# A gated linear-attention and GeGLU kernel rewritten: feature weights folded on chip, numerators issued between the feed-forward matmuls

## The chip, the cores and the metric

The kernel runs on one core of a Trainium2 chip. The metric is the device time of one execution in microseconds (us), as a median over several runs. The one kept profile of the kernel before is of its slow kind: its span of 387.4 us and granted clock of 0.965 are those of its runs near 389 us, while its fastest runs (383 us) had 0.973. Its stages may therefore be some 4 to 6 us too long in sum; in which of them was not measured. "TensorE" is the matrix engine (PE in the profile, PEld its weight loads), "VectorE" is DVE, "ScalarE" is ACT, "GpSimd" is POOL, and SP is the engine whose queue (SPq) issues most transfers. A fast run is one that is not over 1.5% above the fastest of the same kernel; only fast runs enter the ratios.

## The reference

Two branches share one input of 2048 tokens and 640 features, and a sigmoid gate per token mixes them. Branch A is linear attention with 32 heads of 20 features; its feature map is a pair of softmaxes of a small per-head product. Branch B is a feed-forward block with a hidden width of 1728.

```python
qkv = x @ wqkv                                   # q, k, v: 32 heads of 20
pq, pk = q @ w_phi[h], k @ w_phi[h]              # 20 x 20 per head
phi = concat(softmax(p), softmax(-p))            # for pq and pk
kv  = einsum("bhsf,bhsd->bhfd", phi_k, v)        # state: sums over all tokens
z   = phi_k.sum(tokens)
o   = (phi_q @ kv) / (phi_q @ z + 1e-6)          # numerator / denominator
a   = o @ wo
b   = (gelu_tanh(x @ w_gate) * (x @ w_up)) @ w_down
out = g * a + (1 - g) * b                        # g = sigmoid(x . gate_w)
```

The state `kv` needs all tokens, so no numerator can start before the last token's `phi_k`. Branch B depends on none of this.

## The kernel before

It works in three stages with a fence between them: A builds the state, B computes numerators and divides, C runs the feed-forward block and both output products. Heads stand in six groups (five of 6 heads, one of 2), so that a group's 120 features fit 128 rows.

For q, it projects to a feature-major tile, copies it out of PSUM, multiplies by a block-diagonal `w_phi`, and takes two exponentials (k is treated alike in stage A, with a token-major result):

```python
def emit_qT_group(self, b, g):                     # 5 matmuls of 512 columns, then a copy
    ...                                            # (cut)
    sc.compute("act", lambda e: e.activation(self.qTb[0:P, slot, g, :], self.ps[0:P, colQT:colQT + BT], AF.Copy), ...)

def emit_pq_group(self, b, g):
    sc.compute("pe", lambda e: e.matmul(self.ps[0:P, colPQ:colPQ + BT],
        self.BD6[0:P, g, 0:P], self.qTb[0:P, qslot, g, :], start=True, stop=True), ...)
    for s, scale in ((0, 1.0), (1, -1.0)):
        sc.compute("act", lambda e: e.activation(self.eq_ap(b, s, g, ...), self.ps[0:P, colPQ:colPQ + BT], AF.Exp, scale=scale), ...)
```

In stage B each of 16 tiles of 128 tokens gets 12 numerator matmuls, then 24 matmuls of 2 or 6 columns for the softmax denominators and for `phi_q @ z`, then a chain of VectorE operations:

```python
for s in (0, 1):
    for g in range(NG):                            # numerators
        matmul(ps[:, c0:c0 + nh * DA], eq(b, s, g)[tile], self.KVsb[0:P, s, g, 0:nh * DA])
for s in (0, 1):
    for g in range(NG):                            # two narrow products per group
        matmul(ps[:, d0:d0 + nh], eq(b, s, g)[tile], self.G6[0:P, 0:nh])
        matmul(ps[:, z0:z0 + nh], eq(b, s, g)[tile], self.KVz[0:P, s, g, 0:nh])
# emit_tile_dve: 8 small operations on [128, 32], 4 products into O1 and O2, GpSimd adds them into Otm
```

In stage C every chunk of 128 hidden features takes 10 matmuls of 512 columns, and GELU is spelled out:

```python
act(gb, ps_gate, AF.Copy);  act(sq, ps_gate, AF.Square, scale=SQC3);  act(up, ps_up, AF.Copy, scale=0.5)
dve(cube, sq * gb);  dve(u, cube + gb)
act(th, u, AF.Tanh, scale=CT)
dve(h1, (th + 1.0) * gb);  dve(hT, up * h1)
```

The output products of a token block stand between the chunks of the next block, so `hT` has two buffers. `Otm` is transposed on TensorE, five 128x128 transposes per token tile.

The softmax here doesn't subtract the row's maximum and nothing guards it: scores larger than these inputs give would overflow.

## Time and profile before

The median was 384.99 us over three runs (382.83 to 389.44).

First the profile page of the kernel before, its rows of busy tenths. Each digit is the busy share of one of 40 equal slices of the span (9.7 us each); PEclk is the clock granted to TensorE in tenths of full speed.

```profile
PE   2799999974788797669999999999999999999896
DVE  0109999967896969966886155383334751553600
ACT  4157767577164645028996477595555964785522
PEclk9999999999698989589999999999999999999999
```

Up to its last slices, the right half is a row of nines for TensorE at full clock. The left half is not, from the ninth slice on.

Then the stages of the kernel before, from the view of busy time by windows: window, its length, busy us of each engine (instructions), mean granted clock, DMA share, GB/s.

```profile
0.00:14.37 14.37, 4.62 (x26) 2.84 (x26) 1.61 (x6) 4.10 (x5) 5.93 (x28) 1.00 0.69 198
14.37:100.10 85.73, 74.68 (x594) 42.62 (x604) 63.70 (x129) 54.01 (x106) 6.28 (x7) 0.98 0.37 114
100.10:170.90 70.80, 56.90 (x698) 34.60 (x706) 58.94 (x217) 28.61 (x54) 21.95 (x16) 0.85 0.01 2
172.50:384.00 211.50, 208.47 (x1204) 102.86 (x1228) 105.04 (x224) 141.90 (x270) 0.00 (x0) 0.99 0.04 13
```

The columns after the length are PE, PEld, DVE, ACT, POOL. In the last window, the feed-forward stage, TensorE is busy for 208.5 of 211.5 us while ScalarE is busy for 142 and VectorE for 105. In the window of stage B above it, TensorE is busy for 56.9 of 70.8 us and VectorE for 58.9. Neither is full: in the view of waits TensorE stands still there for 4.8 us until VectorE's O products are done and for 6.4 us until ScalarE is (exponentials and q's copies), and VectorE for 6.4 us until TensorE is.

The chain of waits of the kernel before shows the spacing (start, length, what), here two consecutive groups of five gate and up matmuls:

```profile
194.96 1.08 PE psum_arena L892 x5
196.03 1.08 PE psum_arena L886 x5
```

Five matmuls of 512 columns take 1.08 us, 216 ns each. The Trainium skill, "TensorE: Matmul & The Clock Gate", § Back-to-back issue gap, gives N/2.4 + 2.5 ns for N columns, 215.8 ns, as the gap of single matmuls; the trace agrees. "Busy" in the group lines below is the union of overlapping matmuls, so a mean of 380 ns there is the length of one matmul through the pipeline and not its cost.

Last, groups of instructions of the kernel before (line, engine, operation, tiles, shapes, count | busy us, mean ns | idle before and its releasers):

```profile
L754 PE MATMUL psum_arena<-KVz,Eq 128*128 128x6 bf16 x160 | 10.8, 166 | 0.0
L798 DVE TENSOR_TENSOR O_56<-psum_arena,RH 128x480 bf16<-128x480 f32 x16 | 10.4, 651 | 0.0
L734 PE MATMUL psum_arena<-KVsb,Eq 128*128 128x126 bf16 x160 | 14.0, 229 | 4.8 <-DVE O_56 L798 3.3 <-DVE O_57 L803 1.5
L932 DVE SCALAR_TENSOR_TENSOR h1s<-ths,gbs 128x512 bf16<-128x512 bf16 x52 | 36.0, 692 | 82.4 <-ACT ths L931 81.2
L931 ACT ACTIVATE ths<-us 128x512 bf16<-128x512 bf16 x52 | 32.6, 629 | 0.0
```

The third line shows numerators waiting for the O products that empty their PSUM banks. The fourth shows VectorE idle for 82 us before its GELU step: the engines of the elementwise chain wait; TensorE is idle for only 3 of the 211.5 us.

### The profile page before, as it was taken

The page shows a single profiled execution, that of the slowest core. Times are in us where ns is not written, and L with a number is a line of the kernel's source. Part 1 is how long each engine was busy: PE and PEld are TensorE (multiplying, and loading weights), DVE is VectorE, ACT ScalarE, POOL GpSimd, SP SyncE. Part 2 cuts the span into 40 slices and gives each one's busy share as a digit, 9 for nine tenths or more (in the row PEclk, how much of TensorE's full clock was granted, in tenths as well). Part 3 has the DMA queues.
Part 4 walks back from the last instruction along what each step waited for, and adds up shares of the span by engine and source line. Part 5 has one row for each costly group of instructions (what it writes and reads, how often), then busy time and mean ns, then how long its engine had stood idle before and what let it go on. Part 6 is the DMA issues. An engine that isn't in the chain of part 4 may idle for free.

```text
span 387.4 us, 6518 instructions
## 1 busy us (share of the span) xinstructions
PE 344.7 (89%) x2519; PEld 182.9 (47%) x2562; DVE 229.3 (59%) x574; ACT 230.6 (60%) x437; POOL 34.5 (9%) x51
## 2 busy tenths in 40 slices
PE   2799999974788797669999999999999999999896
PEld 1246565542454555524444544445555445444453
DVE  0109999967896969966886155383334751553600
ACT  4157767577164645028996477595555964785522
POOL 6001210000022423420000000000000000000000
PEclk9999999999698989589999999999999999999999
DMA  8445981000000000000000000000000000000010
GB/s 253 95 97 164 339 311 45 2 0 2 0 3 2 2 1 3 2 0 2 0 0 3 17 19 17 19 0 18 18 17 2 17 3 17 19 17 19 0 36 34
DMA packets 15241, 15.60 MB, mean 40 GB/s; under 512 B 9882, under 2 KB 13146, under 8 KB 15210
## 3 DMA queue, kind: packets, MB, share of 16 engines
q1 hardware_dynamic: 13610, 7.73, 7.0%
q0 software_dynamic: 1600, 7.46, 5.7%
q8 instruction: 20, 0.33, 0.4%
q14 instruction: 11, 0.09, 0.1%
HBM read 10.59 MB, written 2.62 MB: 34 GB/s over the span
## 4 chain that ended last, share of the span: by engine, by line
PE 57%; DVE 11%; ACT 8%; issue 2%; POOLq 0%; ACTq 0%; DVEq 0%
PE psum_arena L961 15%; PE psum_arena L886 13%; PE psum_arena L892 12%; PE psum_arena L974 6%; PE psum_arena L654 5%; ACT Eq L688 4%; DVE O_56 L798 2%; DVE O_57 L803 2%; DVE h1s L932 2%; PE psum_arena L945 2%; ACT ths L931 1%; PE psum_arena L520 1%; ACT qTb L661 1%; DVE hT L934 1%; PE psum_arena L734 1%
## 5 line engine op out<-in xcount | busy, mean ns | idle before, releaser
L932 DVE SCALAR_TENSOR_TENSOR h1s<-ths,gbs 128x512 bf16<-128x512 bf16 (+1 forms) x56 | 38.7, 691 | 83.0 <-ACT ths L931 81.8
L886 PE MATMUL psum_arena<-xT,wg_sb 128*128 128x512 bf16 (+1 forms) x274 | 70.6, 387 | 4.1 <-ACT sqs L901 3.5
L892 PE MATMUL psum_arena<-xT,wu_sb 128*128 128x512 bf16 (+1 forms) x274 | 69.1, 382 | 0.2
L961 PE MATMUL psum_arena<-wd_sb,hT 128*128 128x512 bf16 (+3 forms) x439 | 64.9, 298 | 2.0 <-DVE hT L934 1.5
L961 PEld LDWEIGHTS psum_arena<-wd_sb,hT 128*128 128x128 bf16 x448 | 34.2, 98 | 32.2 <-issue 4.0
L899 ACT ACTIVATE gbs<-psum_arena 128x512 bf16<-128x512 f32 (+1 forms) x56 | 33.6, 601 | 19.8 <-POOL Otm L808 18.9
L886 PEld LDWEIGHTS psum_arena<-xT,wg_sb 128*128 128x128 bf16 (+1 forms) x280 | 26.8, 100 | 36.6 <-ACT sqs L901 3.8
L892 PEld LDWEIGHTS psum_arena<-xT,wu_sb 128*128 128x128 bf16 (+1 forms) x280 | 27.9, 100 | 33.8 <-issue 1.6
L948 ACT ACTIVATE goTs<-psum_arena 128x640 bf16<-128x640 bf16 x16 | 11.2, 703 | 53.1 <-PE psum_arena L945 53.1
L931 ACT ACTIVATE ths<-us 128x512 bf16<-128x512 bf16 (+1 forms) x56 | 35.1, 628 | 1.5 <-DVE us L918 1.5
L554 DVE TENSOR_REDUCE DkRk<-Ek 128x64 f32<-128x1280 bf16 x16 | 23.6, 1472 | 20.0 <-ACT Ek L547 20.0
L654 PE MATMUL psum_arena<-xT,wqkv_sb 128*128 128x512 bf16 x111 | 31.5, 431 | 4.0 <-ACT Eq L688 3.3
L904 ACT ACTIVATE ups<-psum_arena 128x512 bf16<-128x512 f32 (+1 forms) x56 | 33.7, 601 | 0.6 <-PE psum_arena L892 0.6
L901 ACT ACTIVATE sqs<-psum_arena 128x512 bf16<-128x512 f32 (+1 forms) x56 | 33.6, 601 | 0.0
L661 ACT ACTIVATE qTb<-psum_arena 128x512 bf16<-128x512 f32 x24 | 14.3, 597 | 32.4 <-PE psum_arena L654 29.7
L808 POOL TENSOR_TENSOR Otm<-O_56,O_57 128x640 bf16<-128x640 bf16 x16 | 22.3, 1395 | 86.7 <-DVE O_57 L803 86.7
L501 PE MATMUL psum_arena<-xT,wqkv_sb 128*128 128x512 bf16 x114 | 29.0, 402 | 0.7 <-DVE BD L465 0.4
L520 PE MATMUL psum_arena<-wqkv_sb,xT 128*128 128x512 bf16 (+1 forms) x157 | 26.3, 297 | 3.0 <-ACT gcol L543 2.9
L688 ACT ACTIVATE Eq<-psum_arena 128x512 bf16<-128x512 f32 x48 | 24.8, 606 | 2.1 <-PE psum_arena L681 2.1
L916 DVE TENSOR_TENSOR cubes<-sqs,gbs 128x512 bf16<-128x512 bf16 (+1 forms) x56 | 23.4, 417 | 3.5 <-ACT sqs L901 3.5
L562 DVE TENSOR_TENSOR Ek<-Ek,DkRk 128x640 bf16<-128x640 bf16 x32 | 25.0, 821 | 0.6
L918 DVE TENSOR_TENSOR us<-cubes,gbs 128x512 bf16<-128x512 bf16 (+1 forms) x56 | 23.8, 424 | 1.9
(77 smaller groups left out, 407.2 us busy)
## 6 DMA issues: line engine op xcount, KB each, us to landing
out_dram<-outsb SPq DMA_DIRECT2D x16, 160.0 KB, 1.8
wd_sb<-in_B_w_down_dram POOLq DMA_DIRECT2D x1, 2080.0 KB, 10.6
wqkv_sb<-in_A_wqkv_dram SPq DMA_DIRECT2D x1, 1600.0 KB, 8.6
wg_sb<-in_B_w_gate_dram POOLq DMA_DIRECT2D x1, 1200.0 KB, 7.6
wu_sb<-in_B_w_up_dram POOLq DMA_DIRECT2D x1, 1200.0 KB, 7.4
wg_sb<-in_B_w_gate_dram POOLq DMA_DIRECT2D x1, 960.0 KB, 7.2
wu_sb<-in_B_w_up_dram POOLq DMA_DIRECT2D x1, 960.0 KB, 5.6
wqkv_sb<-in_A_wqkv_dram SPq DMA_DIRECT2D x1, 800.0 KB
```

Source lines behind the costliest of these rows:

```text
L501: sc.compute("pe", lambda e, kt=kt, last=last, b=b, g=g, col=col: e.matmul(ps[0:P, col:col + BT], self.wqkv_sb[:, kt, D + self.w_col[g]:D ...
L520: sc.compute("pe", lambda e, kt=kt, c0=c0, n=n, last=last, tok0=tok0: e.matmul(ps[:, c0:c0 + n], self.xT[:, kt, tok0:tok0 + P], self.wqkv_ ...
L654: sc.compute("pe", lambda e, kt=kt, last=last, b=b, g=g: e.matmul(self.ps[0:P, colQT:colQT + BT], self.wqkv_sb[:, kt, self.w_col[g]:self.w ...
L688: sc.compute("act", lambda e, s=s, scale=scale, b=b, g=g, colPQ=colPQ: e.activation(self.eq_ap(b, s, g, 0, P, slice(0, BT)), self.ps[0:P, ...
L886: sc.compute("pe", lambda e, kt=kt, last=last, rows=rows, c=c, colg=colg, b=b: e.matmul(ps[0:rows, colg:colg + BT], self.wg_sb[:, kt, c * ...
L892: sc.compute("pe", lambda e, kt=kt, last=last, rows=rows, c=c, colu=colu, b=b: e.matmul(ps[0:rows, colu:colu + BT], self.wu_sb[:, kt, c * ...
L899: sc.compute("act", lambda e, rows=rows, colg=colg: e.activation(gb, ps[0:rows, colg:colg + BT], AF.Copy), reads=[("psb", bg)], writes=[(" ...
L901: sc.compute("act", lambda e, rows=rows, colg=colg: e.activation(sq, ps[0:rows, colg:colg + BT], AF.Square, scale=SQC3), reads=[("psb", bg ...
L904: sc.compute("act", lambda e, rows=rows, colu=colu: e.activation(up, ps[0:rows, colu:colu + BT], AF.Copy, scale=0.5), reads=[("psb", bu)], ...
L931: sc.compute("act", lambda e: e.activation(th, u, AF.Tanh, scale=CT), reads=[("us", cs4)], writes=[("ths", cs2)])
L932: sc.compute("dve", lambda e: e.scalar_tensor_tensor(h1, th, 1.0, gb, ALU.add, ALU.mult), reads=[("ths", cs2), ("gbs", cs4)], writes=[("h1 ...
L961: sc.compute("pe", lambda e, c=c, rows=rows, col=col, n=n, w0=w0, first=first, hslot=hslot, t=t: e.matmul(ps[:, col:col + n], self.hT[0:ro ...
```

## The change

The kernel was rewritten. Its parts, by what each aims at:

1. `w_phi` is folded into `wq` and `wk` on chip (`wq2 = wq @ blockdiag(w_phi)`). Then `pq` and `pk` are single projections of `x`; the copies of q and k and the second products go. k's features come token-major beside v.
2. `phi_q` and the state stand in exactly five tiles of 128 features, heads crossing tile borders; a mask keeps each head's block. Two extra columns per head (a column of ones in v, and the mask itself) give `phi_q @ z` and the softmax denominators inside the numerator matmuls.
3. The numerators are issued between the chunks of the feed-forward stage.
4. The elementwise chain is a native Gelu on ScalarE and one VectorE multiply that reads PSUM. `hT` has one buffer: 14 chunks, then the four output tiles.
5. Normalised outputs are transposed by DMA; wq comes in by transposing loads, as do the later x blocks, now a whole block per load where it was pieces of 512x128. The two half chunks of 64 hidden features share one set of matmuls.

The core of the diff, cut:

```diff
-        emit_kT_group(b, g): kT projection and its copy; emit_v_pk(tau): v and the pk products        (cut)
+    def vk(self, t):                                # v and folded k side by side
+        self.proj(t, 0, 512, 0, 0, ["wv"])
+        self.proj(t, 512, 512, 1, 0, ["wv", "wk2"])
+        self.proj(t, 1024, 257, 2, 0, ["wk2", "wgate"])
+        self.v_evac(t, 0)
+        self.k_evac(t, 0)
...
-            sc.compute("act", ... AF.Copy); ("act", ... AF.Square); ("act", ... AF.Copy, scale=0.5)
-            sc.compute("dve", cube); ("dve", u); ("act", Tanh); ("dve", h1); ("dve", hT)
+            sc.op("act", lambda e: e.activation(self.gl[:, slot, :], self.bank(banks[0]), AF.Gelu_apprx_tanh), ...)
+            sc.op("dve", lambda e: e.tensor_tensor(self.hT[:, c, :], self.bank(banks[1]), self.gl[:, slot, :], ALU.mult), ...)
...
+    def num(self, t):                               # 12 matmuls, 22 columns a head: v, z and the denominator
+        for hf in (0, 1):
+            for s in (0, 1):
+                bk = NBK + 2 * hf + s
+                for r, (i, h0, h1) in enumerate(parts[hf]):
+                    ... e.matmul(self.bank(bk)[:, o0:o0 + n], self.Eq[:, s, i, t * P:(t + 1) * P],
+                        self.KV[:, i, s, k0:k0 + n], start=(r == 0), stop=(r == 2), ...)
+        ...                                         # 8 small VectorE operations, O1, O2, GpSimd adds
+        sc.dma("sp", lambda e: e.dma_start_transpose(self.goT[:, gs, :, :], self.Og[:, sl, :]), ...)
...
+    def ffn(self):
+        for b in range(self.NB):
+            ...
+                order = list(range(14))
+                at = {2: 4 * b + 1, 6: 4 * b + 2, 10: 4 * b + 3}
+            for idx, c in enumerate(order):
+                self.gateup(b, c, pairs[self.pn % 2])
+                if idx in at:
+                    self.num(at[idx])
+            for t in range(4):
+                self.down(4 * b + t, pairs[self.pn % 2])
+                if b < self.NB - 1 and t == 2:
+                    self.num(4 * b + 4)
```

The start of the new kernel matters too. The SP queue issues in this order: two x tiles, wv, two x tiles, wk, one transposed x block, six transposed loads of wq, two transposed x blocks, the other weights. TensorE's program then folds wk, folds wq between four "early" token tiles, and enters a main loop of 12 tiles.

## The prediction

> **What bounds it now.** The view by time slices shows stages: loads and transposes to 14 us; attention state, 14 to 100; numerators and normalisation, 100 to 170; feed-forward, 172 to 384. From 172 us the TensorE row is full (9.95 of every 10 us, clock 1.00), and the chain of waits runs through matmuls spaced 1.08 us per five of 512 columns, 216 ns each. "TensorE: Matmul & The Clock Gate", § Back-to-back issue gap, of the Trainium skill gives N/2.4 + 2.5 ns, 215.8; the trace agrees. ScalarE and VectorE cost nothing there. From 80 to 172 us TensorE is only 40 to 92% busy: it waits for Eq exponentials, qT evictions, Ek normalisation (DVE) and, in the numerators, the O products; the clock falls to 0.7-0.9.
>
> **Removed or moved.** (1) kT/qT projections with their 48 evictions of 0.60 us and the pk/pq products; k comes token-major beside v, phi(q) in five 128-feature tiles (before six). (2) 384 matmuls of 2 or 6 columns (26 ns apart, 10 us): sum columns replace them. (3) The separate numerator stage, 70 us: it moves into the feed-forward stage, where DVE and ScalarE have room. (4) Per chunk, copy, square, tanh and four DVE operations become one Gelu (estimate 0.6 us, like other 128x512 evictions) and one PSUM multiply (estimate 0.65, from 0.65 for 480 PSUM elements): off the critical path, but it makes room for (3). (5) 80 output transposes on TensorE.
>
> **Feed-forward after, estimates.** Gate/up 540 x 216 ns = 116.6 us (the half chunks share matmuls: -4.3). Down and wo: 304 pairs of 320 columns x 272 ns = 82.7. Numerators 16 x 12 matmuls x 66 ns = 12.8. Last gram 1.5. Sum 214 us, against 212 now, TensorE full. A numerator tile's DVE chain (3.6 us plus gaps) fits between two uses of a bank pair.
>
> **Attention after, estimates.** Main loop, 12 tiles: v and k 2.7 us, 1.5 pq groups 1.6, gram 0.8: 5.1 us on TensorE, against ScalarE 4.2 (v copy 0.71, two exponentials 0.73, gate 0.17, pq 1.8) and DVE 3.7. TensorE bound: 61.5 us. Before it, four early tiles with the q fold, one set of banks and 3.7 us of DVE each: 14.5. Before that, a prologue that ends on six transposed loads of wq, behind 2.3 MB of loads and one x block on one queue. Transposed loads now issue at 1.25 us per 512x128 (median; the first took 5.6), so 6.3 for a block and 1.6 for each of wq's: fold of q at 24 to 27 us. TensorE will idle a few us there and lose clock.
>
> **Sum.** 25 + 14.5 + 61.5 + 214 + 3 for the last eviction and store = 318, plus 3 for warm-up, the Gelu table load and stalls: **321 us**, range 311 to 335. Faster by over 2%: 0.97; within 2%: 0.02; slower: 0.01.
>
> **What would show it.** Right: feed-forward starts near 100 us, lasts 212 to 218, TensorE over 95% busy, DVE under 50%; main loop near 5.1 us per tile; the prologue's last wait is a DMA into wqT. Wrong: TensorE waiting in feed-forward for hT or goT (SBUF transposes over 10 us); main loop above 5.6 us, waiting for exponentials or Ek; prologue past 30 us.
>
> **What would make it wrong.** Transposed loads of a whole block, or with wqkv's long row stride, slower than scaled from 512x128 (+5 to 15 us); VectorE's PSUM reads with three free dimensions slower, holding bank pairs after each numerator (+1 us x 16); ScalarE's order making TensorE wait in the main loop (+6); or faster loads and no idle there (-6).

## More of the kernel before

B also holds most of q's projections and exponentials: 18 of the 24 pairs of group and token block; six are in A.

The trace in order of time shows one tile's twelve numerator matmuls, and five matmuls of q's projection a little later:

```profile
121.82 0.78 PE L734 MATMUL psum_arena<-KVsb,Eq 128*128 128x126 bf16 x12
123.04 1.24 PE L654 MATMUL psum_arena<-xT,wqkv_sb 128*128 128x512 bf16 x5
```

## The result, and the profile after

The changed kernel is correct. Its median was 318.56 us (317.17 to 319.37, four runs), against 383.93 us for the kernel before in the same rounds. The ratio of the fast runs is 0.829, with a 95% interval of 0.825 to 0.834. A ratio here is the mean time of one kernel's fast runs over that of the other's of the same rounds, so it is not quite the ratio of the medians. The profiled run is a fast one with a span of 317.7 us.

The rows of busy tenths of the changed kernel, from its profile page:

```profile
PE   4758999999999999999999999999999999999995
DVE  0336998676776667641376540417671044667000
ACT  2533667767676222101222211032221012232010
PEclk9996999999999999999999999999999999999998
```

TensorE is now full from the fifth slice (a slice is 7.9 us here), and ScalarE is nearly idle over the right half. The windows of the changed kernel, with columns as before:

```profile
0.00:23.51 23.51, 13.89 (x127) 8.68 (x129) 5.79 (x11) 8.66 (x12) 6.39 (x41) 0.98 0.87 172
23.51:38.33 14.82, 13.14 (x99) 8.49 (x101) 11.99 (x14) 6.91 (x15) 0.00 (x0) 0.80 1.08 313
38.33:98.38 60.05, 59.60 (x410) 34.34 (x416) 45.46 (x53) 41.93 (x84) 0.00 (x0) 1.00 0.21 69
98.38:313.90 215.52, 214.46 (x1349) 121.76 (x1363) 97.86 (x236) 47.68 (x74) 22.31 (x16) 1.00 0.10 25
```

| Stage | before, us | after, us | predicted, us |
|---|---|---|---|
| loads and preparation | 14.4 | 23.5 | 25 |
| state of k and v, and phi(q): early tiles | in 85.7 | 14.8 | 14.5 |
| state of k and v, and phi(q): main loop | in 85.7 (six of 24 groups of q) | 60.1 | 61.5 |
| numerators and division | 70.8 (with 18 groups of q), and 1.6 of change-over | inside the next stage | inside the next stage |
| feed-forward | 211.5 | 215.5 | 214 |
| last eviction and store | 3.4 | 3.8 | 3 |
| reserve | | | 3 |

The feed-forward stage took in all 16 numerator tiles and its window grew by 4 us (with the two chunks that the kernel before issued in the window of stage B, an estimated 4.3 us, it did not grow). The rest, 172.5 us before, is 98.4 us now. The rows above it don't hold equal work: all of phi(q) is in the early tiles and the main loop now, three quarters of it stood in the 70.8 us before. What was 85.7 + 70.8 us of state, phi(q) and numerators is 74.9 us of state and phi(q), and numerators inside the next stage.

How a numerator tile hides can be read from the trace in order of time, here one tile of the changed kernel (start, length, engine, line, operation):

```profile
160.75 0.85 PE L570 MATMUL ps<-KV,Eq 128*128 128x154 bf16 x12
160.95 0.69 DVE L538 TENSOR_TENSOR hT<-ps,gl 128x512 bf16<-128x512 f32 x1 [1.47 <-PE ps L533]
161.44 1.24 PE L533 MATMUL ps<-xT,wg_sb 128*128 128x512 bf16 x5
161.74 0.36 DVE L586 RECIPROCAL RH<-ps 128x32 f32<-128x32 f32 x1
...
164.54 0.81 DVE L597 TENSOR_TENSOR O_59<-ps,RH 128x640 bf16<-128x640 f32 x1
164.68 1.24 PE L533 MATMUL ps<-xT,wu_sb 128*128 128x512 bf16 x5
164.88 0.60 ACT L536 ACTIVATE gl<-ps 128x512 bf16<-128x512 f32 x1 [1.56 <-PE ps L533]
165.27 1.38 DVE L538 TENSOR_TENSOR hT<-ps,gl 128x512 bf16<-128x512 f32 x2
166.96 1.21 SPq L602 DMA_TRANSPOSE goT<-Og  x1
```

VectorE's chain runs from 161.74 to 165.35. Meanwhile one multiply into `hT` comes due and is done late, together with the next (x2 at 165.27), and TensorE goes on without a gap on the other pair of banks.

And the prologue, from the chain of waits of the changed kernel:

```profile
5.53 7.50 SPq L227
13.09 1.26 SPq L232
14.39 1.27 SPq L232
...
20.45 2.96 DMA wqT<-in_A_wqkv_dram
23.71 2.69 PE ps L358 x10
```

L227 is the transposed x block, L232 the six transposed loads of wq. The chain that ended last starts with that queue and enters TensorE only when wqT has landed. The ten matmuls after it take 2.69 us; the same ten took 1.53 us later, at full clock.

### The profile page after: what moved, and what is told of

Read it like the earlier page. It is cut to its first block, busy times and chain, and to the rows that moved or that the text cites. A ratio compares the mean times of both kernels' runs of the same rounds, so it can differ in the third digit from the quotient of the medians.

```text
span 317.7 us, 4971 instructions
## 1 busy us (share of the span) xinstructions
PE 301.1 (95%) x1978; PEld 173.3 (55%) x2004; DVE 161.1 (51%) x312; ACT 106.0 (33%) x185; POOL 28.7 (9%) x57
## 4 chain that ended last, share of the span: by engine, by line
PE 89%; SPq 6%; ACT 2%; DMA 1%; issue 1%; ACTq 0%
PE ps L533 35%; PE ps L614 20%; PE ps L358 13%; PE ps L620 7%; PE ps L456 6%; PE ps L570 3%; PE ps L430 3%; SPq L227 2%; SPq L232 2%; PE ps L543 1%; ACT Ek L391 1%; DMA wqT<-in_A_wqkv_dram 1%; SPq L219 1%; SPq L222 0%; SPq L216 0%
## 5 line engine op out<-in xcount | busy, mean ns | idle before, releaser
L614 PE MATMUL ps<-wd_sb,hT 128*128 128x320 bf16 x448 | 65.2, 299 | 0.0
L533 PE MATMUL ps<-xT,wu_sb 128*128 128x512 bf16 x253 | 64.2, 379 | 0.7 <-ACT Eq L462 0.2
L533 PE MATMUL ps<-xT,wg_sb 128*128 128x512 bf16 x251 | 62.8, 379 | 0.3
L536 ACT ACTIVATE gl<-ps 128x512 bf16<-128x512 f32 x52 | 31.1, 597 | 83.2 <-PE ps L533 74.2
L538 DVE TENSOR_TENSOR hT<-ps,gl 128x512 bf16<-128x512 f32 x52 | 35.7, 688 | 43.6 <-PE ps L533 43.5
L614 PEld LDWEIGHTS ps<-wd_sb,hT 128*128 128x128 bf16 x448 | 42.3, 98 | 20.6 <-issue 4.2
L358 PE MATMUL ps<-wvk,xT 128*128 128x512 bf16 (+3 forms) x256 | 49.8, 345 | 2.4 <-ACT gcol L394 1.6
L533 PEld LDWEIGHTS ps<-xT,wu_sb 128*128 128x128 bf16 x260 | 25.4, 98 | 31.1 <-issue 0.7
L358 PEld LDWEIGHTS ps<-wvk,xT 128*128 128x128 bf16 x260 | 25.1, 101 | 26.7 <-issue 1.8
L411 DVE TENSOR_TENSOR Ek<-Ek,Dk 128x640 bf16<-128x640 bf16 x32 | 25.0, 822 | 0.6
```

Source lines behind the costliest of these rows:

```text
L358: sc.op("pe", lambda e, kt=kt: e.matmul(self.bank(bank)[:, bcol:bcol + n], self.xT[:, kt, t * P:(t + 1) * P], self.wvk[:, kt, c0:c0 + n], ...
L411: sc.op("dve", lambda e, v=v, r=r: e.tensor_tensor(v, v, r, ALU.mult), reads=[("Rk", se)], writes=[("Ek", se, s)])
L533: sc.op("pe", lambda e, kt=kt, w=w, bk=bk: e.matmul(self.bank(bk), w[:, kt, c * P:(c + 1) * P], xs(kt), start=(kt == 0), stop=(kt == self. ...
L536: sc.op("act", lambda e: e.activation(self.gl[:, slot, :], self.bank(banks[0]), AF.Gelu_apprx_tanh), reads=[("ps", banks[0])], writes=[("g ...
L538: sc.op("dve", lambda e: e.tensor_tensor(self.hT[:, c, :], self.bank(banks[1]), self.gl[:, slot, :], ALU.mult), reads=[("ps", banks[1]), ( ...
L614: sc.op("pe", lambda e, c=c, lo=lo, bk=bk, w0=w0: e.matmul(self.bank(bk, 320), self.hT[lo:P, c, tt * P:(tt + 1) * P], self.wd_sb[lo:P, c, ...
```

## The experiments

Twelve runs were made in three calls, each call on another chip: ten altered kernels, and in two of the calls the changed kernel itself as a yardstick: 318.06 us (316.49 to 319.39) and 317.53 us (316.31 to 319.07). The second call had no yardstick; its kernel before stood at 388.34 us, as in the first (388.16), so I compare it with 318 us and leave differences under 2 us unread. All results were correct.

The theory, from the prediction: the gain is that VectorE's numerator chain now runs under matmuls that fill TensorE anyway, plus fewer matmuls and fewer waits in building the state. Rivals: the native Gelu is the gain; the gain is the smaller number of matmuls wherever they stand.

### after_ref and after_ref2: the yardsticks

> The changed kernel unchanged, as the yardstick on the same chip as the three that follow: 318 to 319 us in the fast state.

> The changed kernel again, as the yardstick on the same chip as the three that follow: 317 to 320 us.

Measured: 318.06 and 317.53 us, as said above.

### b_gelu: the native Gelu alone, in the kernel before

```diff
-            copy, square and scaled copy on ScalarE; cube, u, h1, hT on VectorE; tanh on ScalarE   (cut)
+            sc.compute("act", lambda e, ...: e.activation(gb, ps[0:rows, colg:colg + BT], AF.Gelu_apprx_tanh), ...)
+            sc.compute("dve", lambda e, ...: e.tensor_tensor(
+                self.hT[0:rows, hslot, c, :], ps[0:rows, colu:colu + BT], gb, ALU.mult), ...)
```

> One part of the change alone, in the kernel before: one native Gelu and one multiply from PSUM per chunk in place of copy, square, copy, tanh and four VectorE operations. Theory (TensorE binds the feed-forward stage, the elementwise chain is hidden): 0 to 2 us faster, 382 to 386 us. Rival (ScalarE and VectorE, 60% busy over the span, hold the stage back, and the native Gelu is where the gain comes from): 10 us faster or more.

Measured: 387.03 us (382.10 to 388.52) against 388.34 us (383.00 to 389.88); ratio of the fast runs 0.994, interval 0.980 to 1.009. The kernel before has runs near 383 and near 389, and this one does too; its profile fell among the slower ones and is not used for times. The rival's 10 us (a ratio of 0.974) lies outside the interval. This rests on two fast runs of b_gelu; whether the Gelu alone gains a few us or none is open. Its profile and that of the kernel before are both slow ones, with the same clock of 0.965, and can be set side by side: over 172.5 to 384 us TensorE was busy for 209.3 us (208.5 before), while VectorE fell from 105 to 38.6 us. A chain that is off the critical path was shortened, and about nothing came of it.

### a_oldgelu: the changed kernel with the old elementwise chain

```diff
-            sc.op("act", ... AF.Gelu_apprx_tanh ...);  sc.op("dve", hT = ps_up * gl)
+            self.chain(ps_gate, ps_up, ...)      # copy, square, scaled copy; cube, u; tanh; h1, hT
...
+            self.flush()                         # finish the block's last chunks ahead of its output tiles
             for t in range(4):
                 self.down(4 * b + t, pairs[self.pn % 2])
```

> The changed kernel with the old elementwise chain (three evictions and a tanh on ScalarE, four operations on VectorE) and the numerators still in the feed-forward stage. Theory (the Gelu makes the room for the numerators): in a run of 14 chunks VectorE needs 14 x 1.95 + 3 x 3.9 = 39 us and ScalarE 14 x 2.43 = 34, against 32 us of TensorE, so TensorE waits for hT and for banks, and the time rises by 25 to 45 us, to 343 to 363 us. Rival 1 (it would all have been hidden here too): at most 3 us more. Rival 2 (the Gelu is most of the gain): over 60 us more.

Measured: 370.58 us (369.70 to 371.27), ratio to before 0.960: about 52 us more than the changed kernel. The direction was the theory's, the size was above its range. The trace of this run, waits of TensorE in the feed-forward stage (engine, line, what it waited for: us in total, times, longest):

```profile
PE ps L650 <- DVE hT L571: 14.2, 12, 2.9
PE ps L534 <- ACT sqs L555: 11.4, 5, 2.5
PE ps L650 <- ACT sqs L555: 11.0, 3, 3.8
PE ps L606 <- DVE O L633: 2.0, 2, 1.2
```

L650 is the output product, which now waits for `hT`; L534 is gate and up, which waits for banks that the square on ScalarE frees. These are 38.6 us of waits; the profiled run's mean clock was 0.963, against 0.987 for the changed kernel, and over the stage (98 to 365 us) TensorE was busy for 227.3 us, 12.8 us more than the 214.5 of the changed kernel. The waits and this together are 51.4 of the 52 us. The changed kernel has, in the same view of the same stage, one line:

```profile
PE ps L533 <- ACT Eq L462: 0.2, 1, 0.2
```

So the same elementwise operations that were hidden in the kernel before cost 52 us here. That left a question: is it the engine time, or the new order with 14 chunks in a row and one `hT` buffer? (The copy is not exact: this version keeps square, cube, sum, tanh and h1 in one scratch tile of four slots, where the kernel before has five tiles. ScalarE's square waits 10.2 us for a slot's `hT` here and 12.0 us in the next run; what that costs was not tested.)

### a_oldgelu2: the old chain in the old order

```diff
-            [("hT", [P, NFC, BT], BF16), ("gbs", [P, 4, BT], BF16)],
+            [("hT", [P, 2, NFC, BT], BF16), ("gbs", [P, 4, BT], BF16)],
...
+                at = {1: 4 * b - 1, 5: 4 * b, 8: 4 * b + 1, 12: 4 * b + 2}
+                dn = {3: 4 * b - 4, 4: 4 * b - 3, 7: 4 * b - 2, 10: 4 * b - 1}
...
+                if idx in dn:
+                    down(dn[idx])
                 if idx in at:
                     self.num(at[idx])
-            self.flush()
-            for t in range(4): ...
+        self.flush()
+        self.num(15)
+        for t in range(12, 16):
+            down(t)
```

> The old elementwise chain in the changed kernel again, now in the order of the kernel before: the four down products of a block stand between the chunks of the next block, with two hT buffers. The first try (14 chunks in a row, one hT buffer) cost 52 us. Theory A (what the native Gelu pays for is the engine time: VectorE has 27 us of chain and 15.6 us of numerators per 53 us of TensorE, which fits when spread): 3 to 15 us over the changed kernel, 321 to 333 us, so most of the 52 us came from the order, which only a short chain allows. Theory B (the engine time itself does not fit beside the numerators): 30 us or more, 348 us or more.

Measured: 340.78 us (340.48 to 343.36), ratio 0.884: 23 us over the yardstick of its call. Neither theory's range holds it. Spreading the output tiles, with the second `hT` buffer that this needs, took back about 30 of the 52 us, so the larger part was order and buffer together. The other 23 us stay although neither engine is full; this window holds the body of the stage in this run:

```profile
130.00:310.00 180.00, 167.72 (x1035) 92.86 (x1032) 139.94 (x314) 106.38 (x196) 21.64 (x14) 0.99 0.09 24
```

VectorE is busy for 140 of 180 us (78%) and ScalarE for 106 (59%), and TensorE still loses 12 us there. My expectation added up engine time and allowed too little for chains in which ScalarE and VectorE hand a chunk back and forth behind a numerator of 3.6 us in the same in-order queue. The waits in the trace are of that kind (7.9 us for the square, 5.6 us for `hT`, 4.0 us for the O products), but no run separates them further.

### a_numstage: the numerators in a stage of their own

```diff
-            [("goT", [P, 6, KD, P], BF16), ...
+            [("goT", [P, 16, KD, P], BF16), ...
-        NBK = self.NUMB
+        NBK = 4 * (t % 2)
...
+        self.gram(14)
+        self.gram(15)
+        self.kv_evac()
+        self.gates()
+        for t in range(self.NT):
+            self.num(t)
         for b in range(self.NB):
-            (the gram, kv_evac, gates and num calls between chunks and output tiles: cut)
```

> The changed kernel with all 16 numerator tiles in a stage of their own ahead of the feed-forward stage, two sets of four banks in turn. Theory (the gain comes from hiding VectorE's numerator chain under full TensorE work): the stage lasts 16 x 3.9 = 62 us plus 8 us to fill, the feed-forward stage loses 13 us of numerator matmuls, so 50 to 62 us more, 368 to 381 us. Rival (the gain is in the smaller number of matmuls, wherever they stand): under 10 us more.

Measured: 371.91 us (371.12 to 373.50), ratio 0.964: 54 us more than the changed kernel, inside the theory's range and far from the rival's. Some 3 us of it are not the numerators' own: the end of the state, hidden between chunks in the changed kernel, now stands alone, and the stage begins at 101.4 us where feed-forward began at 98.4. Its windows: numerators, then feed-forward.

```profile
101.40:161.50 60.10, 24.02 (x194) 19.16 (x193) 55.33 (x175) 0.00 (x0) 20.89 (x15) 0.51 0.21 42
161.50:365.60 204.10, 204.06 (x1148) 109.91 (x1148) 38.81 (x56) 45.33 (x71) 1.39 (x1) 0.99 0.04 14
```

VectorE is busy for 55 of 60 us in the first window, TensorE for 24 at half its clock, in the second TensorE is full. The same instructions, moved, cost 54 us: in their own stage they are VectorE time, and between chunks they are 11 us of TensorE time.

### a_tiny: the narrow matmuls put back

```diff
                 bk = NBK + 2 * hf + s
+                for r in range(6):
+                    i = (2 * hf + r) % 5
+                    sc.op("pe", lambda e, ...: e.matmul(
+                        self.bank(bk)[:, 400 + 8 * r:406 + 8 * r], self.Eq[:, s, i, t * P:(t + 1) * P],
+                        self.KV[:, i, s, 0:6], start=True, stop=True, skip_group_check=True), ...)
```

> In the changed kernel, the 24 six-column matmuls per token tile that the sum columns replaced are put back (their results are not used). Theory (TensorE is full in the feed-forward stage, so every matmul added there is paid in full, and these run 26 ns apart): 384 x 26 ns = 10 us more, about 328 us. Rival (there is slack beside the numerators' waits): less than 3 us more.

Measured: 327.25 us (325.35 to 328.66), 9.2 us over the yardstick of its call, 24 ns for each of 384 matmuls. The Trainium skill, "TensorE: Matmul & The Clock Gate", § Wait — 56ns, not 53.3ns?, says that start-to-start never drops below about 25 ns however few columns a matmul has; this run's trace agrees, with most of the 384 at 25 ns from start to start. In a stage where TensorE is full, each added matmul is paid in full.

### a_petr and a_petr2: the output transposes back on TensorE

```diff
-        sc.dma("sp", lambda e: e.dma_start_transpose(self.goT[:, gs, :, :], self.Og[:, sl, :]), ...)
+        for c in range(self.KD):                   # tp(), five transposes into the first numerator bank
+            sc.op("pe", lambda e, c=c: e.transpose(pv[:, c * P:(c + 1) * P], self.Og[:, sl, c * P:(c + 1) * P], self.ident[:, :]), ...)
+        sc.op("act", lambda e: e.activation(self.goT[:, gs, :, :], pv..., AF.Copy), ...)
```

In a_petr, `tp()` of one tile comes directly ahead of the numerator matmuls of the next.

> The changed kernel with the output transposes back on TensorE (5 per token tile, 64 ns apart, evicted by ScalarE) in place of the DMA transposes. Theory: 80 x 64 ns = 5 us more plus a little waiting, 323 to 326 us. Rival (the DMA transposes cost nothing and gain nothing, TensorE has slack): within 1 us.

Measured: 339.49 us (337.87 to 340.24), about 21 us more, four times the expectation. The waits of TensorE in this stage are one line:

```profile
PE ps L571 <- ACT goT L614: 13.8, 15, 1.3
```

The transposes share a bank with the numerators behind them, so TensorE stood still while ScalarE emptied it, 0.9 us fifteen times. a_petr2 issues `tp()` one chunk, or one output tile, earlier:

```diff
             for idx, c in enumerate(order):
+                if idx in at:
+                    self.tp()
...
             for t in range(4):
+                if t == 2 or (b == 0 and t == 0):
+                    self.tp()
                 self.down(4 * b + t, pairs[self.pn % 2])
```

> TensorE output transposes again, now issued one chunk or one tile ahead of the next numerator instead of directly ahead of it. In the first try TensorE waited 13.8 us in all, 0.8 to 1.3 us per numerator, for ScalarE to empty the bank that the transposes share with the numerators. Theory (that wait was made by the place of the transposes and is not their cost): the wait goes and 5 to 8 us over the changed kernel are left, 323 to 327 us. Rival (transposes on TensorE cost what the first try showed, 20 us): 335 us or more.

Measured: 326.73 us (326.06 to 327.54), 9.2 us over the yardstick of its call. The rival falls; the sum was 1 us short. The old wait is gone and a smaller one is there:

```profile
PE ps L611 <- POOL Og L600: 3.2, 3, 1.2
```

The 64 ns of the expectation was read too high: in the trace of the kernel before, the starts of a tile's five transposes are mostly 56 ns apart, 58 in the mean. 80 of them are 4.7 us and this wait is 3.2 us, together 7.9 of the 9.2. So the DMA transposes are worth some 9 us here.

### a_actload: more ScalarE work in the main loop

```diff
         self.v_evac(t, 0)
+        (the same copy of v once more)
         self.k_evac(t, 0)
```

> The changed kernel with the v copy on ScalarE done twice in each of the 12 tiles of the main loop, 0.71 us more per tile. Theory (TensorE binds the loop at 5.1 us per tile, ScalarE needs 4.2): under 1.5 us more. Rival (ScalarE binds the loop, or is so close that its order stalls TensorE): 12 x 0.71 = 8.5 us more.

Measured: 318.11 us (317.16 to 319.68), 0.6 us over the yardstick of its call, which is inside the scatter. ScalarE's busy time between 40 and 100 us rose from 42.2 us in the yardstick of its call to 50.3 us, as this window shows, and TensorE stayed full:

```profile
40.00:100.00 60.00, 59.47 (x412) 33.81 (x410) 44.83 (x51) 50.34 (x97) 0.00 (x0) 1.00 0.17 57
```

The main loop is bound by TensorE.

### a_wqfirst: wq's transposed loads first

```diff
-        xblock(1)
         for g, (h0, nh) in enumerate(self.GH):
             (transposed load of wqT group g)
+        xblock(1)
         xblock(2)
         xblock(3)
```

> Only the order of the loads is changed: the six transposed loads of wq go ahead of the transposed load of the second x block. Theory (the prologue ends on a wait for wqT, and the clock falls because of it): the wait at 21 to 23.5 us goes, the granted clock of 20 to 30 us stays near 1, and the time falls by 3 to 5 us against the changed kernel. Rival (the early tiles are bound by ScalarE, VectorE and one set of banks, so an earlier wqT only waits): less than 1 us.

Measured: 314.93 us (313.09 to 316.10), 3.1 us under the yardstick of its call. In the yardstick TensorE's first early k tile started at 22.8 us, in this run at 19.9 us, and the line of a wait for wqT is gone from TensorE's waits. The part of the expectation about the clock failed: over 20 to 34 us the mean granted clock (after the five busy times in the windows below) was 0.88 in both runs. First the yardstick, then this run, then the next one, a_tuned:

```profile
20.00:34.00 14.00, 9.81 (x70) 6.20 (x71) 8.81 (x11) 4.57 (x10) 0.00 (x0) 0.88 0.99 247
20.00:34.00 14.00, 12.16 (x101) 8.18 (x98) 11.67 (x14) 7.19 (x16) 0.00 (x0) 0.88 1.09 309
20.00:34.00 14.00, 12.20 (x109) 7.92 (x107) 11.72 (x14) 8.92 (x19) 0.00 (x0) 1.00 1.07 287
```

The gain is the earlier start, and not the clock. In these two profiles the wait for wqT is 1.7 of the 2.9 us; the yardstick had also waited longer for its first x tiles (4.4 against 3.6 us), which this order doesn't touch.

### a_tuned: also a fuller early section

```diff
-        self.fold(0, "q", (4, 5), "dve")
         self.k_early(0, 0)
-        (the other folds of q between the early tiles, all evicted by VectorE; pq from the third tile on: cut)
+        self.fold(0, "q", (6, 7), "dve")
+        self.fold(1, "q", (4, 5), "dve")
+        self.fold(2, "q", (6, 7), "act")
+        self.fold(3, "q", (4, 5), "dve")
+        self.fold(4, "q", (6, 7), "act")
+        self.k_norm(0)
+        self.k_early(1, 0)
+        self.pq(0, 0, 0)
+        ...                                        # pq(0, 1) and pq(0, 2) behind the next two tiles
```

> The same order of loads, and also: the first early k tile ahead of the q fold, two of the five q fold evictions on ScalarE, and one phi(q) group between each pair of early k tiles, so that TensorE has work while one set of banks is being read. Theory: TensorE fills the early section, 5 to 8 us less than the changed kernel. Rival (VectorE's four normalisations and evictions bind there): no better than the new order of loads alone, within 1 us.

Measured: 313.44 us (313.06 to 315.75), 4.6 us under the yardstick and 1.5 us under a_wqfirst. It is the fastest kernel here, 0.814 of the kernel before (interval 0.809 to 0.819). It missed its range by a little and lies between the theory and the rival. The main loop starts at the same time as in a_wqfirst (34.0 against 33.8 us), with one phi(q) group more behind it: those are the 1.1 us of five matmuls. The order did not shorten the section itself, although the granted clock over 20 to 34 us was 1.00 here against 0.88: VectorE was busy for 11.7 of the 14 us in both runs, which speaks for the rival, but no run took VectorE work away, so that stays argued.

## Why the prediction was right

The predicted time was 321 us with a range of 311 to 335; measured were 318.56 us. Point by point:

- **What bound the kernel before.** TensorE in feed-forward, waits between engines before it. b_gelu agrees: with 66 us less of VectorE work in that stage TensorE was as busy as before, and no gain clear of noise came of it.
- **The numerator stage.** The prediction moved it where VectorE has room. a_numstage shows it: 54 us for the move alone. Its "separate numerator stage, 70 us" was read too simply, since 18 groups of q stood in that window too; the sum did not suffer, because it was built from the new kernel's own tiles and not by taking 70 us away.
- **The Gelu.** "Off the critical path, but it makes room": both halves were right, and the room was worth more than I would have said. Alone it gave 0.6%, with 0 and 2% both inside the interval; without it the new kernel loses 23 us in a spread order and 52 us in its own. The gains of parts 3 and 4 therefore can't be added. The kernel before with the Gelu alone kept its time (0.994); the changed kernel without the Gelu stands at 0.960; the changed kernel without the move at 0.964; with both, 0.829.
- **Feed-forward.** 215.5 us against 214. Two terms were off and by luck partly cancelled. Down and wo take 3.91 + 1.46 = 5.37 us per tile, 85.9 us in all, against 82.7. The spacing of the 320-column matmuls was right: 136 ns from start to start in the trace. What was left out is the half chunk: its two matmuls use 64 rows of the array and not 128, and at the change to 64 rows the next start comes after 231 ns, at the change back after 228, in all 16 tiles: 0.19 us per tile, 3 us in all. The view of waits has it as idle time of the weight loads (us in total, times, longest):

```profile
PEld ps L614 <- issue: 4.2, 16, 0.3
PEld ps L620 <- issue: 4.2, 16, 0.3
```

The other term: the 12 numerator matmuls take 0.69 us, 11.0 us in all, against 12.8. TensorE was busy for 99.5% of the stage and VectorE for 45%, as predicted. a_tiny shows that it binds.
- **Main loop.** 60.05 us for 12 tiles, 5.0 us each against 5.1. a_actload shows the slack of ScalarE.
- **Prologue.** The last wait was for wqT, as said, and ended at 23.5 us against 24 to 27. The terms inside were off: a transposed x block was scaled to 6.3 us from pieces of 128 KB; the first took 7.5 us behind the loads ahead of it, and the two later ones together 5.40 us, 2.7 each. a_wqfirst shows what this order of the loads cost: 3 us.
- **The reserve of 3 us** was not needed: the time at a lower clock (0.80 granted) sits inside the 14.8 us of the early tiles, which had been estimated without it. That the stages' errors all stayed under 2 us is in part luck.
- **Transposes.** The prediction listed the 80 output transposes as removed, without a figure; the expectation of a_petr put them at 5 us. a_petr2 puts the part at 9 us, since without the DMA a wait comes with them.

What folding `w_phi` (part 1) and the five full tiles (part 2) gained was not split by experiments. The windows put together give only this: 85.7 us of state with six groups of q became 74.9 us of state with all of phi(q), while the prologue grew by 9 us.

## What to carry to other kernels

An engine that is full in one stage is the place to hide another engine's work from a stage where it isn't: price the moved work at what it costs the full engine (11 us here), not at what it takes in a stage of its own (60 us). Shortening an elementwise chain under a full TensorE gained nothing clear of noise by itself here, but test it again once other work has moved in beside it, because the same operations that were free before cost 23 to 52 us after, in the form in which they were put back here. And when a part put back costs several times its instructions, look at which bank or buffer it shares before believing the number: its place in the order was most of it (21 us against 9).

## What the Trainium skill lacked or had wrong

- "TensorE: Matmul & The Clock Gate", § Back-to-back issue gap, gives a measured sustained spacing in real kernels of about 131 ns per matmul at N = 512 and says that the formula N/2.4 + 2.5 over-counts there. In these streams, each matmul with its weight load, it is 216 ns (five in 1.08 us), and 136 ns at N = 320 (start to start in the changed kernel's down products), as the formula has it (215.8 and 135.8).
- The same page, § Part 4: PE-mode transpose, gives about 275 ns for one 128x128 transpose in a kernel and says that the full clock does not engage for it. In the feed-forward stage of the kernel before, at a granted clock of 0.99, 80 of them took 221 ns each from start to end (the profile models the ends), like the plain 128-column matmuls there (219 ns), and started mostly 56 ns apart. They stand between other matmuls, so what a run of transposes alone does to the clock is not shown.
- "DMA: Bandwidth & Descriptors", § Latency and other measured facts, has 261 GB/s for transposing DMAs with a non-contiguous middle dimension and about 350 to 400 for contiguous ones, without sizes. By issue time on the queue, pieces of 512x128 (128 KB) went at 1.26 us each, 104 GB/s; blocks of 512x640 (640 KB) at 2.70 us each, 243 GB/s. It has no transfer time for a transpose from SBUF to SBUF: 128x640 landed 2.6 us after issue (median of 16).
- "ScalarE: Activation LUTs", § What ACT_TABLE_LOAD costs, gives 1283 ns for the load, as both traces show, plus a drain of about 1380 ns. At the one switch in the changed kernel's main body, from Exp to Gelu, the load began 0.01 us after the last Exp ended (99.68 us) and the first Gelu began at 100.97 us; no drain beside the load is to be seen.
